# Two issuing queues for the loads, and a new order of words, in a fused RWKV-6 and gated state-space kernel

## Chip, cores, metric

The kernel runs on one core of one Trainium2 chip. The metric is the device time of one execution in microseconds (us). Below, PE is TensorE, PEld its weight loads, DVE VectorE, ACT ScalarE, POOL GpSimd and SP SyncE. The granted clock is the share of TensorE's full clock that the chip let it have. An engine "stands" when it is idle because its next instruction may not start yet.

## The reference

For 4 batches of 768 steps and 8 heads of 48 values, the first half is a recurrence with a decay per step (RWKV-6); its output x, 384 wide, goes through a projection, a linear scan, a gate and a second projection.

```python
for t in range(S):                                     # r, k, v, w: [4, 8, 768, 48]
    cur = np.einsum('bhd,bhe->bhde', u[None] * kt, vt)
    y[:, :, t] = np.einsum('bhd,bhde->bhe', rt, state + cur)
    state = wt[:, :, :, None] * state + np.einsum('bhd,bhe->bhde', kt, vt)
...
proj = x @ w_in                                        # 384 -> 2 x 512
val, gate = proj[..., :D_inner], proj[..., D_inner:]
for t in range(S):
    h = a[0, 0] * h + val[:, t, :]
    ys[:, t, :] = h
silu = gate * (1.0 / (1.0 + np.exp(-gate)))
return silu * ys @ w_out
```

## The kernel before

The sequence is cut into 12 segments of 256 steps (two chunks of 128). Everything the kernel does is a word of one long list; the words run through a small interpreter, and each engine executes its own words strictly in list order. `ld.4.w` loads w of segment 4, `ld.4.v.1` one half of v, `lw` a part of a weight matrix; `Q`, `K`, `ru`, `vc`, `dv` are products and casts whose letter after the colon names the engine (d, p or a); `y.6` is DVE's sum of chunk 6; `op`, `osb`, `ship` are the last product, its copy out of PSUM and its transfer to the output.

```python
ORDER = """
ld.0.w.1 ld.0.w.0 ldu ld.0.k.1 ld.0.r.1 ln.0.1 cs.0.P.1:0 ld.0.k.0 cs.0.N.1:1 ex.0.P.1 ln.0.0
ld.0.r.0 ex.0.N.1 tot.0:2 cs.0.P.0:0 ld.1.w cs.0.N.0:1 ex.0.P.0 Q.0.1:d ex.0.N.0 E.0 K.0.1:d
... (54 lines cut; 733 words in all)
"""
class InOrder:                       # each engine keeps the order of the list
    def __getattr__(self, name):
        op = getattr(self.engine, name)
        return lambda *args, **kwargs: self.tc.keep_in_program_order(op(*args, **kwargs))
...
    qp = ring("qp", NB, [C, G, H, DP], BF16)
    kp = ring("kp", NB, [C, G, H, DP], BF16)
    loaded = {x: ring(x, 6, [C, G, H, D], F32) for x in "rkvw"}
...
    def ld_(m, name, g=None):
        T[name, m] = loaded[name][m % 6]
        if g is None:                # w: a whole segment, runs of 384 bytes
            sp.dma_start(out=pairs(T[name, m]), in_=...)
            return
        sp.dma_start(out=T[name, m][:, g], in_=...)   # a half: runs of 192 bytes
...
    for word in ORDER.split():
        word, _, place = word.partition(":")
        fn, *args = word.split(".")
        ...
        work[fn](*(int(a) if a.isdigit() else a for a in args), **given)
```

Of the kernel before, what the change touches and what calls it, by code (L numbers as in the profile page):

```python
# [528 lines left out]
```

## Time and profile before

| | before |
|---|---|
| median of 3 runs | 151.3 us (150.02 to 151.83) |
| span of the profiled run, mean granted clock | 149.1 us, 0.973 |
| busy us: PE, DVE, ACT, POOL | 121.3, 123.2, 104.3, 87.7 |

### The profile page before, as it was taken

How to read it: one execution, taken by the hardware profiler on the slowest of the kernel's cores; microseconds unless marked ns; L12 is line 12 of the kernel's file. 1: busy time of each engine (PE TensorE's matmuls, PEld its weight loads, DVE VectorE, ACT ScalarE, POOL GpSimd, SP SyncE). 2: the span in 40 equal slices, each digit the busy share in tenths (PEclk: the TensorE clock that was granted, in tenths of full speed). 3: DMA queues.
4: the chain of work that ended last, by engine and by line, in shares of the span. 5: the costliest groups of instructions: out<-in, count | busy, mean ns of one | idle time of the engine just before them, and what ended most of it. 6: DMA issues, size and time to landing. Idle time of an engine off the chain costs nothing.

```text
span 149.1 us, 3917 instructions
## 1 busy us (share of the span) xinstructions
PE 121.3 (81%) x1560; PEld 83.8 (56%) x1560; DVE 123.2 (83%) x171; ACT 104.3 (70%) x186; POOL 87.7 (59%) x82
## 2 busy tenths in 40 slices
PE   0436985759996779998879799999697999999990
PEld 0124643435574546786547578777444677777760
DVE  3049649998559999899999999999869999989930
ACT  3725566845858898799968899889544785655471
POOL 7801627059629939687139699629699429194100
PEclk9999999999999999999999999999857999999998
DMA  4999999999799999899898998999991211301235
GB/s 93 193 228 202 202 159 257 228 205 255 135 206 206 167 234 254 174 209 313 164 208 185 210 199 180 276 203 197 241 254 38 98 67 52 110 0 57 106 135 181
DMA packets 94690, 26.40 MB, mean 177 GB/s; under 512 B 89424, under 2 KB 94672, under 8 KB 94672
## 3 DMA queue, kind: packets, MB, share of 16 engines
q1 hardware_dynamic: 94672, 26.16, 85.1%
q8 instruction: 12, 0.20, 0.7%
q14 instruction: 6, 0.05, 0.1%
HBM read 21.43 MB, written 4.72 MB: 175 GB/s over the span
## 4 chain that ended last, share of the span: by engine, by line
PE 31%; SPq 26%; DVE 20%; DMA 9%; issue 6%; ACT 3%; POOL 3%; DVEq 0%; ACTq 0%; POOLq 0%
SPq L100 26%; PE mm L100 20%; PE yk L100 6%; DVE rk L100 6%; DVE hT L100 5%; DVE At L100 4%; DMA r<-in_r_dram 4%; DMA v<-in_v_dram 3%; PE trp L100 3%; DMA k<-in_k_dram 3%; DVE y L100 2%; PE att L100 2%; DVE kp L100 1%; POOL kp L100 1%; ACT z L100 1%
## 5 line engine op out<-in xcount | busy, mean ns | idle before, releaser
L100 PE MATMUL mm<-xT,w_in_sb 128*128 128x256 bf16 x288 | 38.1, 277 | 1.5 <-DVE hT L100 0.7
L100 PEld LDWEIGHTS <-w_in_sb 128*128 128x128 bf16 x288 | 26.9, 99 | 7.1 <-issue 3.3
L100 DVE TENSOR_TENSOR At<-att,mask 128x1024 bf16<-128x1024 f32 x24 | 29.1, 1212 | 0.6 <-PE att L100 0.6
L100 ACT COPY QK<-trp 128x1024 bf16<-128x1024 bf16 x24 | 24.3, 1012 | 7.2 <-PE trp L100 6.9
L100 POOL TENSOR_TENSOR qp<-r,P 128x768 bf16<-128x768 f32 x10 | 19.4, 1940 | 15.9 <-DMA r<-in_r_dram 11.0
L100 POOL TENSOR_TENSOR dv<-v,dvec 128x768 f32<-128x768 f32 x12 | 18.3, 1526 | 9.4 <-DMA v<-in_v_dram 3.5
L100 DVE TENSOR_TENSOR_SCAN hT<-a_f,hT,mm 128x256 bf16<-128x256 f32 x32 | 22.5, 732 | 0.4 <-issue 0.2
L100 PE MATMUL mm<-w_out_sb,z 128*128 128x384 bf16 x96 | 20.0, 342 | 2.1 <-DVE z L100 1.0
L100 ACT COPY osb<-mm 128x384 f32<-128x384 f32 x24 | 11.3, 478 | 11.6 <-PE mm L100 11.5
L100 DVE TENSOR_TENSOR y<-yk,dv 128x384 bf16<-128x384 f32 x24 | 13.1, 545 | 5.9 <-PE yk L100 5.8
L100 PEld LDWEIGHTS <-QK 48*128 48x128 bf16 x352 | 11.5, 101 | 11.2 <-issue 8.2
L100 POOL TENSOR_TENSOR rk<-r,u_b 128x768 f32<-128x768 f32 x8 | 15.2, 1901 | 3.8 <-DMA r<-in_r_dram 3.8
L100 POOL TENSOR_TENSOR kp<-k,N 128x768 bf16<-128x768 f32 x8 | 15.6, 1954 | 2.5 <-DMA k<-in_k_dram 2.5
L100 DVE TENSOR_TENSOR rk<-rk,k 128x768 f32<-128x768 f32 x12 | 17.0, 1417 | 0.1
L100 ACT ACTIVATE z<-mm 128x512 bf16<-128x512 f32 x24 | 14.1, 601 | 3.4 <-PE mm L100 3.1
L100 ACT COPY xT<-trp 128x384 bf16<-128x384 bf16 x24 | 11.5, 479 | 6.8 <-PE trp L100 6.7
L100 PEld LDWEIGHTS <-kp 128*48 128x48 bf16 (+1 forms) x256 | 11.5, 109 | 8.0 <-issue 5.1
L100 PE MATMUL att<-QK 48*128 48x128 bf16 x192 | 11.0, 243 | 4.3 <-DVE At L100 3.2
L100 PE MATMUL mm<-lwp,triP 64*128 64x384 bf16 (+1 forms) x46 | 8.1, 412 | 7.3 <-ACT lwp L100 6.8
L100 ACT ACTIVATE lwp<-w 128x768 bf16<-128x768 f32 (+1 forms) x13 | 10.3, 795 | 4.8 <-DMA w<-in_w_dram 4.7
L100 PEld LDWEIGHTS <-z 128*128 128x128 bf16 x96 | 9.0, 100 | 7.9 <-issue 2.5
L100 ACT ACTIVATE P<-mm 128x384 f32<-128x384 f32 x24 | 10.9, 492 | 3.3 <-PE mm L100 3.2
(54 smaller groups left out, 201.4 us busy)
## 6 DMA issues: line engine op xcount, KB each, us to landing
k<-in_k_dram SPq DMA_DIRECT2D x24, 192.0 KB, 4.8
r<-in_r_dram SPq DMA_DIRECT2D x24, 192.0 KB, 5.0
v<-in_v_dram SPq DMA_DIRECT2D x24, 192.0 KB, 4.6
out_dram<-osb SPq DMA_DIRECT2D x24, 192.0 KB, 2.5
w<-in_w_dram SPq DMA_DIRECT2D x11, 384.0 KB, 5.0
stage<-in_moe_w_in_dram SPq DMA_DIRECT2D x4, 384.0 KB, 5.9
stage<-in_moe_w_out_dram SPq DMA_DIRECT2D x2, 384.0 KB, 5.5
w<-in_w_dram SPq DMA_DIRECT2D x2, 192.0 KB, 3.0
```

The source lines that it names most:

```text
L100: return lambda *args, **kwargs: self.tc.keep_in_program_order(op(*args, **kwargs))
```

## The change

Its intent: SP's queue holds every transfer and runs back to back (gaps of 0.04 us) to about 112 us; if ACT issues the loads of w, two queues feed the DMA. The list was worked out anew for this, with load times measured on the chip.

```diff
 ORDER = """
-ld.0.w.1 ld.0.w.0 ldu ld.0.k.1 ld.0.r.1 ln.0.1 cs.0.P.1:0 ld.0.k.0 cs.0.N.1:1 ex.0.P.1 ln.0.0
-ld.0.r.0 ex.0.N.1 tot.0:2 cs.0.P.0:0 ld.1.w cs.0.N.0:1 ex.0.P.0 Q.0.1:d ex.0.N.0 E.0 K.0.1:d
+ld.4.w lda ld.2.w ld.0.w.0 ld.0.w.1 ldu ld.0.r.1 ld.0.r.0 ln.0.0 ld.0.k.0 ln.0.1 cs.0.P.1:0
+ld.6.w ld.1.w cs.0.N.0:1 ld.0.v.0 ex.0.P.1 cs.0.N.1:2 ld.3.w cs.0.P.0:0 ex.0.N.1 Q.0.1:d
 ... (the whole list is new: the same 733 words in another order, 19 of K, Q, ru, dv, vc, z, cw on another engine)
-    qp = ring("qp", NB, [C, G, H, DP], BF16)
-    kp = ring("kp", NB, [C, G, H, DP], BF16)
+    qk = ring("qk", NB, [C, G, 2, H, DP], BF16)
+    qp, kp = [[t[:, :, i] for t in qk] for i in range(2)]
+    W_ON_ACT = (1, 2, 3, 4, 5, 6, 7, 8, 9, 10, 11)
 ...
-            sp.dma_start(
+            (act if m in W_ON_ACT else sp).dma_start(
                 out=pairs(T[name, m]),
```

(A word for a transposing DMA was added too; the list does not use it.)

More of the change, by code (lines that the diff above doesn't have):

```diff
@@ L23 @@
 ORDER = """
-ld.0.w.1 ld.0.w.0 ldu ld.0.k.1 ld.0.r.1 ln.0.1 cs.0.P.1:0 ld.0.k.0 cs.0.N.1:1 ex.0.P.1 ln.0.0
-ld.0.r.0 ex.0.N.1 tot.0:2 cs.0.P.0:0 ld.1.w cs.0.N.0:1 ex.0.P.0 Q.0.1:d ex.0.N.0 E.0 K.0.1:d
-ld.0.v.0 tr.1 ld.0.v.1 ru.0:d QK.1 ld.1.r.1 Q.0.0:d sc.1 rk.0 ln.1 ld.2.w K.0.0:d cs.1.P:01
-red.0 tr.0 ld.1.r.0 ex.1.P.0 vc.0:p At.1 ex.1.P.1 ld.1.k.0 dv.0:p QK.0 adv.0 cs.1.N:20 ld.1.k.1
-S.1 out.1 ln.2 ld.2.r.1 sc.0 y.1 tot.1:1 ex.1.N.0 Q.1:p At.0 ld.2.r.0 adv.1 E.1 yT.1 ld.2.k.1
-xT.1 S.2 out.0 ex.1.N.1 tot.2:1 ld.3.w cs.2.N:02 K.1:d ex.2.N.0 y.0 tr.2 ex.2.N.1 ld.4.w
@@ L30 @@
-cs.2.P:02 ru.2:d QK.2 ru.1:d ld.2.k.0 ex.2.P.0 tr.3 ex.2.P.1 sc.2 rk.1 ld.1.v.1 E.2 ln.3 Q.2:p
-ld.1.v.0 red.1 QK.3 cs.3.P:02 At.2 lw.0 ex.3.P.0 yT.0 tot.3:1 ex.3.P.1 rk.2 ld.3.r.1 E.3
-cs.3.N:02 xT.0 sc.3 ln.4 K.2:d ld.3.r.0 ex.3.N.0 tot.4:1 dv.1:p red.2 ld.2.v.0 tr.4 vc.1:a At.3
-ld.6.w E.4 out.2 ex.3.N.1 QK.4 cs.4.P:10 cw.0:d adv.2 ld.2.v.1 ex.4.P.0 tr.5 y.2 Q.3:p sc.4
-ex.4.P.1 S.3 lw.1 At.4 QK.5 adv.3 cs.4.N:20 ld.3.k.0 out.3 ru.3:p ex.4.N.0 sc.5 ex.4.N.1 y.3
-yT.2 ld.3.k.1 ln.6 At.5 lda vc.2:p xT.2 cs.6.P:10 S.4 pv.0.0:2 ex.6.P.0 dv.2:p ld.5.w yT.3
@@ L36 @@
-cw.1:a out.4 adv.4 ex.6.P.1 ld.4.r.0 y.4 pv.0.1:0 af K.3:p xT.3 scn.0.0 ld.4.r.1 yT.4 pv.1.1:1
-scn.0.2 xT.4 S.5 ld.4.k.1 scn.0.1 tr.6 scn.0.3 ln.5 ld.3.v.0 rk.3 QK.6 cs.5.N:20 ld.4.k.0 out.5
-scn.1.2 ex.5.N.0 tr.7 Q.4:p ld.3.v.1 sc.6 scn.1.3 ex.5.N.1 QK.7 cs.6.N:02 ld.7.w y.5 pv.1.0:1
-red.3 ru.4:p ex.6.N.0 yT.5 ld.4.v.0 At.6 ex.6.N.1 xT.5 cs.5.P:02 ld.4.v.1 scn.1.0 ex.5.P.0 sc.7
-K.4:p ex.5.P.1 ld.5.r.0 scn.1.1 vc.3:a tot.6:0 tot.5:2 ld.5.r.1 E.6 rk.4 ln.7 tr.8 ld.8.w dv.3:p
-QK.8 red.4 cs.7.N:10 adv.6 out.6 ex.7.N.0 S.7 tr.9 At.7 lw.3 dv.4:p ex.7.N.1 adv.7 E.5 cs.7.P:01
@@ L42 @@
-QK.9 ld.5.k.0 y.6 sc.8 tot.7:2 S.8 vc.4:p out.7 ex.7.P.0 At.8 ld.5.k.1 yT.6 E.7 ex.7.P.1 Q.5:p
-pv.2.1:2 ln.8 lw.2 y.7 scn.2.2 xT.6 cs.8.N:01 ld.6.r.0 cw.3:a yT.7 scn.2.3 out.8 ru.5:p sc.9
-ex.8.N.0 y.8 ld.6.r.1 adv.8 xT.7 pg.2.1:2 S.9 ex.8.N.1 At.9 ld.5.v.0 adv.9 K.5:p sl.2.1 pv.3.0:0
-ld.5.v.1 S.10 out.9 scn.3.0 yT.8 pv.2.0:1 ld.6.k.1 rk.5 xT.8 pg.0.1:2 cw.2:a scn.3.1 ld.6.k.0
-Q.6:p tr.10 sl.0.1 scn.2.0 pg.1.0:0 lw.5 QK.10 y.9 pg.2.0:2 red.5 vc.5:p lw.4 sl.1.0 yT.9 sc.10
-scn.2.1 xT.9 pg.0.0:0 ru.6:p sl.2.0 ld.9.w At.10 pg.1.1:1 sl.0.0 cs.8.P:20 sl.1.1 z.2:d ld.7.r.1
@@ L48 @@
-out.10 ex.8.P.0 rk.6 tot.8:1 adv.10 ld.7.r.0 tr.11 z.0:d ld.6.v.0 z.1:d E.8 ex.8.P.1 pv.3.1:1
-K.6:d cw.5:a ld.7.k.1 pv.4.1:0 cw.4:a scn.3.2 dv.5:p ld.7.k.0 S.11 QK.11 op.5:2 scn.4.2 ld.6.v.1
-ru.7:p scn.3.3 osb.5 tr.12 ln.9 ld.7.v.0 op.3:2 y.10 scn.4.3 op.1:1 QK.12 ld.8.r.1 Q.7:d tot.9:0
-sc.11 osb.1 yT.10 ld.10.w rk.7 osb.3 op.4:1 E.9 xT.10 cs.9.N:20 At.11 vc.6:p osb.4 tr.13
-ld.8.r.0 ex.9.N.0 pv.4.0:1 K.7:p red.6 ex.9.N.1 ld.8.k.1 adv.12 QK.13 cs.9.P:02 scn.4.0 sc.12
-ld.7.v.1 out.11 ex.9.P.0 dv.6:p S.13 tr.14 y.11 ld.8.k.0 ex.9.P.1 At.12 QK.14 op.0:0 ld.11.w
@@ L54 @@
-Q.8:p adv.13 ln.10 scn.4.1 sc.13 yT.11 out.12 S.14 osb.0 ld.9.k.0 cs.10.N:21 At.13 xT.11 op.2:0
-vc.7:p ex.10.N.0 ld.9.r.0 tr.15 y.12 osb.2 K.8:p ex.10.N.1 red.7 tot.10:0 ld.9.r.1 sc.14 E.10
-cs.10.P:12 QK.15 At.14 pv.5.1:0 ld.8.v.1 dv.7:p adv.14 ex.10.P.0 yT.12 ld.8.v.0 scn.5.2 sc.15
-ex.10.P.1 out.14 xT.12 At.15 pg.3.1:1 ru.8:p ld.9.k.1 ln.11 pv.5.0:2 y.14 sl.3.1 ship.5 tr.17
-scn.5.3 ld.11.k.1 Q.9:p out.13 scn.5.0 pg.5.1:0 ship.0 S.15 QK.17 pg.3.0:1 ship.2 scn.5.1
-ld.10.r.0 y.13 sl.5.1 pg.4.0:2 rk.8 sl.3.0 yT.13 ld.10.k.1 out.15 sl.4.0 z.3:d pg.5.0:0
@@ L60 @@
-ld.10.r.1 xT.13 ru.9:d sc.17 sl.5.0 tr.16 ship.4 op.7:1 vc.8:a At.17 K.9:p ld.10.k.0 adv.15
-QK.16 pg.4.1:2 y.15 ld.9.v.0 op.6:0 S.16 sl.4.1 rk.9 ld.10.v.0 tr.18 osb.6 sc.16 red.8 Q.10:p
-osb.7 pg.6.0:2 ld.11.k.0 QK.18 pv.6.1:0 At.16 ld.9.v.1 sl.6.0 yT.14 pg.6.1:1 dv.8:p red.9 xT.14
-ld.10.v.1 yT.15 sl.6.1 adv.16 scn.6.2 tot.11:2 ship.7 xT.15 out.16 K.10:p S.17 E.11 ship.3 sc.18
-scn.6.3 tr.19 ld.11.r.0 y.16 pv.6.0:1 At.18 QK.19 vc.9:p cs.11.P:02 ld.11.v.1 out.17 z.5:d
-ex.11.P.0 tr.20 ld.11.r.1 adv.18 scn.6.0 ru.10:p ex.11.P.1 sc.19 QK.20 ld.11.v.0 op.11:0 S.19
@@ L66 @@
-scn.6.1 adv.19 ship.6 osb.11 y.17 yT.16 cs.11.N:21 xT.16 ship.1 rk.10 out.18 op.10:0 ex.11.N.0
-ship.11 z.4:d ex.11.N.1 tr.21 osb.10 pv.7.1:1 dv.9:p At.19 QK.21 op.8:2 scn.7.2 op.9:0 z.6:p
-osb.8 y.18 vc.10:a sc.20 ship.8 yT.17 scn.7.3 pg.7.0:2 osb.9 At.20 pv.7.0:1 xT.17 ship.9 sl.7.0
-K.11:p ship.10 pg.7.1:0 S.20 scn.7.0 out.19 adv.20 red.10 yT.18 sl.7.1 op.12:2 Q.11:p scn.7.1
-xT.18 sc.21 pv.8.0:0 osb.12 y.19 vc.11:a ship.12 pv.8.1:1 S.21 scn.8.0 z.7:p yT.19 pg.8.0:2
-scn.8.2 xT.19 out.20 scn.8.1 sl.8.0 tr.22 At.21 pg.8.1:0 QK.22 dv.10:p adv.21 scn.8.3 op.13:2
@@ L72 @@
-S.22 sc.22 ru.11:p osb.13 tr.23 y.20 op.14:1 ship.13 At.22 adv.22 osb.14 out.21 rk.11 QK.23
-ship.14 pg.9.1:2 y.21 pv.9.1:1 sl.8.1 red.11 out.22 sl.9.1 sc.23 S.23 yT.20 dv.11:p pg.9.0:0
-scn.9.2 xT.20 At.23 pv.9.0:2 sl.9.0 z.8:p yT.21 op.15:0 y.22 xT.21 scn.9.3 out.23 osb.15 yT.22
-pg.10.0:1 y.23 ship.15 xT.22 scn.9.0 yT.23 pv.10.0:0 sl.10.0 scn.9.1 xT.23 op.17:1 scn.10.0
-z.9:p pv.11.0:2 osb.17 scn.10.1 op.16:1 scn.11.0 pv.10.1:0 osb.16 scn.11.1 pg.10.1:1 ship.16
-scn.10.2 ship.17 pg.11.0:2 sl.10.1 scn.10.3 pv.11.1:1 sl.11.0 z.10:d op.18:0 scn.11.2 pg.11.1:2
@@ L78 @@
-osb.18 scn.11.3 op.20:0 ship.18 sl.11.1 op.19:1 osb.20 z.11:d op.21:2 ship.20 osb.19 op.22:0
-ship.19 osb.21 op.23:1 ship.21 osb.22 ship.22 osb.23 ship.23
+ld.4.w lda ld.2.w ld.0.w.0 ld.0.w.1 ldu ld.0.r.1 ld.0.r.0 ln.0.0 ld.0.k.0 ln.0.1 cs.0.P.1:0
+ld.6.w ld.1.w cs.0.N.0:1 ld.0.v.0 ex.0.P.1 cs.0.N.1:2 ld.3.w cs.0.P.0:0 ex.0.N.1 Q.0.1:d
+ex.0.P.0 tot.0:2 ru.0:d E.0 ex.0.N.0 ld.0.k.1 K.0.0:d Q.0.0:d ld.0.v.1 tr.0 ld.1.k.0 QK.0
+ld.1.r.0 sc.0 ln.1 K.0.1:d ld.1.k.1 rk.0 af tr.1 cs.1.N:02 ld.1.r.1 red.0 vc.0:p ex.1.N.0 At.0
@@ new lines @@
+ex.1.N.1 adv.0 QK.1 cs.1.P:10 S.1 dv.0:d tot.1:2 ld.5.w out.0 E.1 ex.1.P.0 adv.1 y.0 K.1:p sc.1
+ex.1.P.1 yT.0 ld.1.v.0 At.1 ld.1.v.1 ru.1:d ln.3 Q.1:d ld.2.r.0 xT.0 cs.3.P:20 rk.1 ld.2.r.1
+tot.3:1 tr.2 ln.2 red.1 lw.0 out.1 E.3 QK.2 tot.2:1 ld.2.k.1 ex.3.P.0 tr.3 dv.1:d ex.3.P.1 sc.2
+ld.2.k.0 QK.3 y.1 vc.1:p cs.2.P:02 At.2 lw.1 ex.2.P.0 yT.1 ru.2:p ex.2.P.1 S.2 sc.3 xT.1 adv.2
+At.3 ld.9.w cs.2.N:02 cw.0:a out.2 Q.2:p ex.2.N.0 ld.3.r.1 y.2 ex.2.N.1 S.3 yT.2 E.2 adv.3
+ld.8.w ld.3.r.0 rk.2 xT.2 cs.3.N:02 out.3 K.2:d ex.3.N.0 ld.3.k.1 pv.0.0:1 cw.1:a red.2 ld.3.k.0
@@ new lines @@
+tr.4 ln.4 scn.0.0 ld.2.v.1 ex.3.N.1 y.3 QK.4 pv.0.1:0 scn.0.1 ld.2.v.0 cs.4.P:21 Q.3:p scn.0.2
+ld.10.w yT.3 sc.4 lw.3 xT.3 scn.0.3 ld.7.w ex.4.P.0 S.4 tot.4:0 At.4 tr.5 ex.4.P.1 K.3:p E.4
+cs.4.N:12 QK.5 pv.1.0:0 ld.4.r.0 ex.4.N.0 scn.1.0 tr.6 vc.2:p sc.5 ld.4.r.1 scn.1.1 QK.6 dv.2:p
+out.4 At.5 lw.2 cw.3:a sc.6 ru.3:p ex.4.N.1 y.4 tr.7 ln.5 At.6 QK.7 cs.5.P:01 ld.4.k.0 adv.4
+rk.3 pv.1.1:2 ex.5.P.0 S.5 Q.4:p yT.4 ld.4.k.1 ex.5.P.1 sc.7 xT.4 tot.5:0 At.7 out.5 ld.3.v.1
+pg.0.1:1 cw.2:a scn.1.2 ru.4:p ld.5.r.1 E.5 pg.0.0:0 ln.6 y.5 scn.1.3 yT.5 ld.3.v.0 sl.0.1 red.3
@@ new lines @@
+pg.1.1:2 ld.5.r.0 K.4:d xT.5 pg.1.0:1 ld.4.v.1 rk.4 sl.0.0 tr.8 sl.1.1 ld.4.v.0 pv.2.0:0 z.0:d
+sl.1.0 QK.8 cs.6.P:21 z.1:d scn.2.0 vc.3:p ex.6.P.0 red.4 lw.4 dv.3:p out.6 adv.6 tr.9 scn.2.1
+ld.11.w lw.5 ex.6.P.1 S.7 y.6 QK.9 adv.7 cs.5.N:01 Q.5:d ld.5.k.0 sc.8 out.7 ex.5.N.0 vc.4:p
+At.8 tot.6:2 ex.5.N.1 yT.6 ld.5.k.1 E.6 cs.6.N:01 ln.7 dv.4:p S.8 ld.6.r.0 y.7 adv.8 xT.6
+tot.7:2 S.9 ex.6.N.0 out.8 cw.4:d ld.6.r.1 sc.9 E.7 ex.6.N.1 At.9 ru.5:p cs.7.P:20 cw.5:a yT.7
+adv.9 ex.7.P.0 op.1:1 y.8 ex.7.P.1 K.5:d osb.1 ld.6.k.1 cs.7.N:02 xT.7 op.3:1 rk.5 ex.7.N.0
@@ new lines @@
+ld.6.k.0 tr.11 osb.3 S.10 ex.7.N.1 pv.3.0:1 Q.6:p red.5 ld.5.v.0 QK.11 pv.2.1:0 scn.3.0 ld.5.v.1
+tr.10 scn.2.2 ln.8 out.9 ru.6:p ld.7.r.1 scn.3.1 op.0:2 QK.10 scn.2.3 op.2:1 ld.7.r.0 osb.0 y.9
+yT.8 pg.2.0:0 osb.2 K.6:d xT.8 ld.6.v.0 pv.3.1:2 sl.2.0 rk.6 tr.12 sc.10 scn.3.2 vc.5:p pg.3.0:1
+At.10 QK.12 pg.2.1:0 dv.5:p ld.6.v.1 adv.10 sl.3.0 scn.3.3 sc.11 yT.9 ld.7.k.1 sl.2.1 pg.3.1:1
+Q.7:p At.11 xT.9 cs.8.P:20 ld.7.k.0 sl.3.1 out.10 S.11 red.6 ex.8.P.0 tr.13 ru.7:p sc.12 y.10
+tot.8:1 At.12 out.11 E.8 ld.8.r.1 QK.13 pv.4.0:1 vc.6:p y.11 ex.8.P.1 ld.8.r.0 yT.10 scn.4.0
@@ new lines @@
+dv.6:p adv.12 xT.10 out.12 S.13 cs.8.N:02 ln.9 scn.4.1 ld.8.k.0 sc.13 adv.13 K.7:p ex.8.N.0
+yT.11 y.12 tot.9:1 ld.7.v.1 xT.11 At.13 E.9 ln.10 pg.4.1:1 ld.7.v.0 z.2:d yT.12 ex.8.N.1 rk.7
+xT.12 pv.4.1:0 ld.8.k.1 sl.4.1 out.13 S.14 ru.8:p scn.4.2 ld.9.r.0 op.4:2 red.7 tr.15 ld.9.k.1
+osb.4 pv.5.0:1 Q.8:p QK.15 scn.4.3 op.5:2 ship.0 scn.5.0 vc.7:a tr.14 ld.8.v.0 y.13 pg.5.1:0
+osb.5 z.3:d ld.9.r.1 sc.15 QK.14 pg.5.0:2 scn.5.1 K.8:p At.15 sl.5.1 ld.8.v.1 yT.13 pg.4.0:1
+sl.5.0 rk.8 xT.13 cs.9.P:02 sc.14 sl.4.0 adv.14 dv.7:p At.14 ex.9.P.0 pv.6.0:1 ld.10.r.1 tr.16
@@ new lines @@
+S.15 out.14 scn.6.0 ru.9:p ship.2 adv.15 ex.9.P.1 scn.6.1 ld.9.k.0 QK.16 cs.10.P:02 y.14
+pv.6.1:1 ld.9.v.1 z.4:d ex.10.P.0 yT.14 out.15 scn.6.2 vc.8:p ex.10.P.1 sc.16 ship.1 xT.14
+cs.9.N:02 S.16 Q.9:p scn.6.3 ld.10.k.1 tr.17 ex.9.N.0 adv.16 At.16 ln.11 op.7:1 ld.9.v.0
+ex.9.N.1 S.17 osb.7 rk.9 op.8:0 ld.10.r.0 QK.17 tot.11:2 y.15 K.9:p op.9:1 ld.11.r.0 red.8 osb.8
+yT.15 out.16 E.11 osb.9 ld.10.k.0 red.9 cs.11.N:02 xT.15 sc.17 dv.8:p tot.10:1 ex.11.N.0 At.17
+tr.18 ship.7 E.10 ex.11.N.1 pv.7.0:1 ship.4 QK.18 vc.9:p y.16 cs.10.N:02 ship.5 scn.7.0 out.17
@@ new lines @@
+ex.10.N.0 ru.10:p ld.10.v.1 yT.16 adv.18 ex.10.N.1 scn.7.1 sc.18 xT.16 cs.11.P:02 ship.9 S.19
+pv.5.1:1 At.18 ship.3 ex.11.P.0 K.10:p tr.19 ex.11.P.1 ld.11.r.1 adv.19 scn.5.2 QK.19 pg.7.1:0
+ld.11.v.1 y.17 dv.9:p pv.7.1:2 sl.7.1 scn.5.3 sc.19 ship.8 yT.17 scn.7.2 op.6:1 ld.11.k.0 Q.10:p
+At.19 out.18 osb.6 pg.7.0:0 ld.11.v.0 xT.17 pg.6.1:1 scn.7.3 sl.7.0 ld.10.v.0 z.5:d tr.21 sl.6.1
+pv.8.0:2 z.7:d QK.21 ld.11.k.1 pg.6.0:0 rk.10 tr.20 ship.6 sl.6.0 y.18 Q.11:p op.10:1 scn.8.0
+QK.20 out.19 scn.8.1 op.15:0 z.6:p sc.20 y.19 osb.15 yT.18 pv.8.1:2 At.20 osb.10 xT.18 op.14:0
@@ new lines @@
+vc.10:a S.20 op.11:1 red.10 K.11:p yT.19 sc.21 osb.11 scn.8.2 adv.20 osb.14 ship.11 out.20 At.21
+xT.19 pg.8.1:1 dv.10:p tr.22 scn.8.3 pv.9.1:0 QK.22 S.21 vc.11:p pg.8.0:2 y.20 sl.8.1 scn.9.2
+sc.22 ru.11:p adv.21 sl.8.0 tr.23 S.22 op.12:1 At.22 QK.23 op.13:2 rk.11 osb.12 out.21 osb.13
+yT.20 sc.23 z.8:p scn.9.3 ship.13 pg.9.0:1 y.21 ship.12 pv.9.0:2 sl.9.0 red.11 ship.10 pg.9.1:0
+xT.20 ship.14 scn.9.0 yT.21 dv.11:p op.16:1 sl.9.1 scn.9.1 xT.21 adv.22 At.23 out.22 z.9:p
+pg.10.1:0 y.22 pg.10.0:2 sl.10.1 S.23 yT.22 out.23 sl.10.0 pv.10.1:0 osb.16 y.23 xT.22 op.19:2
@@ L80 @@
+scn.10.2 yT.23 pv.10.0:1 osb.19 scn.10.3 xT.23 op.18:2 scn.10.0 pv.11.0:0 osb.18 scn.10.1
+op.17:2 ship.18 scn.11.0 z.10:p ship.19 pv.11.1:1 osb.17 scn.11.1 ship.15 pg.11.0:2 ship.17
+scn.11.2 pg.11.1:0 sl.11.0 ship.16 scn.11.3 op.20:2 sl.11.1 op.21:1 z.11:d osb.20 ship.20
+op.22:0 osb.21 ship.21 op.23:2 osb.22 ship.22 osb.23 ship.23
 """
@@ L223, in ld_ @@
         t = {"r": r, "k": k, "v": v, "w": w}[name]
+        b, s = divmod(m, NS)
         if g is None:
-            b, s = divmod(m, NS)
-            sp.dma_start(
+            (act if m in W_ON_ACT else sp).dma_start(
                 out=pairs(T[name, m]),
@@ L349, in dv, with trd @@
             T["d", m].unsqueeze(2).to_broadcast([C, G * H, D]))
+    def trd(n):
+        m, g = divmod(n, G)
+        T["QK", n] = t = QKs[n % 3]
+        sp.dma_start_transpose(
+            out=t.rearrange("r i p c -> r (i p) c"),
+            in_=qk[m % NB][:, g].rearrange("t i h d -> t (i h d)"))
     def tr(n):
@@ L487 @@
         ld=ld_, ldu=ldu, lda=lda, lw=lw, cw=cw, af=af, ln=ln, cs=cs, ex=ex, tot=tot, E=E, K=K, Q=Q,
-        vc=vc, rk=rk, ru=ru, red=red, dv=dv, tr=tr, QK=QK, sc=sc, At=At, adv=adv, S=S, out=out_,
+        vc=vc, rk=rk, ru=ru, red=red, dv=dv, tr=tr, trd=trd, QK=QK, sc=sc, At=At, adv=adv, S=S, out=out_,
         y=y, yT=yT, xT=xT, pv=pv, scn=scn, pg=pg, sl=sl, z=z, op=op, osb=osb, ship=ship)
```

## The prediction

The "6 loads" are ACT's table loads. Rival A lost its counterargument so: it was not shown (in the changed kernel 6 of ACT's 11 issues found none of its own loads under way). Sum: from a span of 149.1 us it comes to 148.2 and then 146.9 us, with 2.2 us more for an unprofiled run to 149.1, and 148.9 was said. Its 0.7 us is an estimate from the trace of before, where rk, z, ru and kp on DVE took 10.3 us over their undisturbed times in 29 operations, all of it in nine that ran beside an operation of POOL's. That the stop at 107 us brought the half clock, on which 3.4 of its 4.8 us rest, was assumption: the trace shows the two together (a stop of 1.39 us to 107.21, half clock from 107.0 us), not that one makes the other. The "15 to 16 ns" are the median of the 192 B packets in that trace, 15 ns (mean 18).

> **What bounds the kernel now.** I read the page first, then the busy times by stretches, then the chain of waits in order of time, and last the DMA queue and TensorE around the places that the chain named. From the page, five lines:
>
> ```profile
> PE 121.3 (81%) x1560; PEld 83.8 (56%) x1560; DVE 123.2 (83%) x171; ACT 104.3 (70%) x186; POOL 87.7 (59%) x82
> ...
> DVE  3049649998559999899999999999869999989930
> ...
> PEclk9999999999999999999999999999857999999998
> DMA  4999999999799999899898998999991211301235
> ...
> PE 31%; SPq 26%; DVE 20%; DMA 9%; issue 6%; ACT 3%; POOL 3%; DVEq 0%; ACTq 0%; POOLq 0%
> ```
>
> No engine is over 83%, but the digits show who is full when: the DMA from slice 1 to slice 29 (a slice is 3.73 us, so to about 112 us), DVE from slice 9 to slice 29, and at the end DMA is nearly idle and DVE has 6 to 9 tenths. The busy times by stretches (length; then PE, PEld, DVE, ACT, POOL; clock, DMA share, GB/s) make this exact:
>
> ```profile
> 8.00:20.00 12.00, 8.21 (x105) 5.32 (x105) 8.28 (x13) 5.90 (x10) 4.07 (x3) 1.00 1.26 208
> 20.00:34.00 14.00, 9.62 (x94) 5.21 (x92) 12.70 (x12) 9.20 (x18) 5.45 (x3) 1.00 1.15 216
> 34.00:60.00 26.00, 22.32 (x333) 15.04 (x333) 21.70 (x32) 20.72 (x41) 19.36 (x13) 1.00 1.11 208
> 60.00:90.00 30.00, 27.14 (x394) 20.29 (x395) 29.08 (x40) 26.38 (x45) 20.73 (x15) 1.00 1.01 204
> 90.00:107.00 17.00, 15.07 (x228) 11.80 (x226) 16.97 (x22) 14.70 (x24) 10.84 (x7) 1.00 1.01 224
> 107.00:119.00 12.00, 10.60 (x93) 6.34 (x93) 9.96 (x10) 5.92 (x11) 10.14 (x6) 0.72 0.56 134
> 119.00:146.00 27.00, 26.55 (x318) 19.30 (x315) 23.11 (x36) 17.27 (x32) 11.01 (x6) 1.00 0.24 84
> ```
>
> So there are three stages: loads and their latency to about 34 us; DVE from 34 to 107 us (67.75 busy of 73); PE from 107 to 146 us. The hinge is at 107 us. In the chain of waits and then in PE's timeline (start, length, engine, operation) it reads:
>
> ```profile
> 101.50 4.68 DMA v<-in_v_dram
> 106.26 0.08 issue
> 106.34 0.83 POOL vb L100
> ```
>
> ```profile
> 105.58 0.25 PE L100 MATMUL yk<-s_zero,ident 128*128 128x192 bf16 x1
> 107.21 0.36 PE L100 MATMUL yk<-vb,kp 128*48 128x48 bf16 x8 [1.39 <-POOL vb L100]
> 107.50 0.61 PE L100 MATMUL att<-QK 48*128 48x128 bf16 x8
> 108.04 1.46 PE L100 MATMUL mm<-w_out_sb,z 128*128 128x384 bf16 x4
> ```
>
> A v half for segment 9 lands late, PE stands for 1.39 us, and the clock records put a granted clock of 0.5 from 107.0 to 113.8 us: the four matmuls of one output tile take 1.46 us there and 0.82 later. From 107 us on, PE hardly stops again.
>
> [...] successive r, k and v halves (192 KB) land about 1.0 us apart, a whole w (384 KB, half as many packets a byte) about 1.5 us, and where a 16 KB instruction fetch from another queue falls (19.3, 34.6, 58.6 us) landings slip by about 1 us. [...] the product rk on DVE takes 0.95 us alone and 2.78 us at 110.5 us, when a POOL product runs until 112.4. [...] the trace's 6 loads took 7.7 us, 1283 ns each.
>
> **The change part by part.**
> *Issue.* Eleven w loads leave SP's queue for ACT's. SP issues of a load take 0.43 to 0.57 us while the queue is empty (the first four) and about 1.0 us on average when it is full, which is back-pressure, since landings are 1.0 us apart as well. SP has gaps of 0.04 us only and 4 to 5 loads under way, so nothing is gained from a faster issuer. ACT pays 11 x about 0.55 = 6 us (an estimate from those first issues). The sequence of exponentials and silu switches set 8 times instead of 6: 2 x 1.28 = 2.6 us. Three casts of v leave ACT for POOL: 3 x 0.83 = 2.5 us less. ACT goes from 104 to about 110 us: still not the bound.
> *Load stream.* Same bytes[...]: it should still end at 110 to 113 us. What changes is the order. Nine shipments instead of six stand before the last load (+3 x 0.5 us), but the late segments' v come in better: the second v half of segment 9 has about ten loads behind it, not five.
> *Start.* ACT issues w of segments 4 and 2 at once, and 6, 1 and 3 as soon as segment 0's logarithms have gone through: 7.5 us of transfers beside SP's. Adding up 1.0 and 1.5 us per load, I put the first r half at about 10.5 us (8.2 now) and the second k half of segment 0 at 18 to 19 us (7.3 now). DVE is then some 5 us behind at 19 us. But it idles now between 20 and 34 us as well, and in the new list has products (ru, Q, dv of segments 0 and 1) to fill the same stretch. Tracing both lists by hand to 34 us, DVE has done 19.0 us of instructions now and about 18.2 after: +0.8 us.
> *DVE.* Counts: ru 4 to 2, Q and K one more each, dv 0 to 2: two more operations of 0.94 us, +1.9 us. [...] rk, z, ru and kp on DVE cost about 10 us over their undisturbed times in some 30 operations, so two more cost about 0.7 us.
> *Tail.* From the first matmul that needs v of segment 9, PE's instructions in list order add up to 33.6 us at full clock; it took 107.2 to 145.6 = 38.4 us. Half clock for 6.8 us is 3.4 us of that, and the stop before it 1.4 us: 4.8 us to be had if this v is early. In the new list the last loads have only 21.3 us (the first user of segment 10's v) and 19.7 us of PE work (the first transposes of k of segment 11) behind them: landing at 112 us, they end PE at about 134 us at the earliest and so bound nothing.
> *Sum.* Span 149.1 + 0.8 + 1.9 + 0.7 - 4.8 x about 0.9 = 148.2; and half of the 2.7 us that DVE idles between 40 and 50 us, mostly for a matmul result, goes with better placed loads: **146.9 us**. The unprofiled median is 2.2 us above the profiled span, which gives 149.1; I say **148.9 us**.
>
> **Rivals.**
> *A: ACT becomes a bound.* If an issue on ACT has to queue behind SP's blocked one, it costs 1 us or more, not 0.55: 11 us or more in an engine that is at 26.4 of 30 us between 60 and 90 us and stands before every decay and every copy out of PSUM. For: SP's issues stretch to 2.7 us. [...] It would make 152 to 154 us.
> *B: the early w crowd out r and k.* Then DVE never makes good its 5 us, because it has only 10 us of idle time from 20 us to its end at 143.8. For: DVE is 93% busy from 34 to 107 us. It would make 151 to 153 us.
> *C: the two queues do raise throughput*, the list fits the measured times, and the loads end some us sooner, at 105 to 108 us. Against: packets of 192 B take 15 to 16 ns an engine, back to back. It would make 144 to 147 us.
> *D: nothing moves*: another late load stops PE elsewhere and brings the half clock again. It would make 150 to 152 us.
>
> **Range and chances.** The clock episode is worth 3% in one piece, and whether one occurs is near a coin toss leaning to no. With it gone and DVE's additions absorbed, 146 to 149; with it, or under A or B, 151 to 154; C gives the low end. The 8 in 10 range is 145 to 153. Faster by over 2% means under 148.3, just below my value: 0.42. Within 2%: 0.45. Slower: 0.13, as A and B would have to come together.
>
> **What would show it.** Right: last r, k or v landing at 110 to 113 us; the k half for segment 0 near 18 us; ACT issues of about 0.55 us; 8 table loads; DVE 124 to 126 us busy; no half clock after 60 us and no PE wait over 1 us for a v there. Wrong: ACT issues over 1 us (A), DVE under 85% between 20 and 50 us (B), last landing before 108 us (C), a new half clock in the tail (D).

## More of the kernel before

The views that bound this kernel stand in the prediction. Here are only the three rows that the result will be held against: busy times by stretches of 20 us. The columns are the stretch and its length, then the busy us (and instructions) of PE, PEld, DVE, ACT and POOL, the granted clock, the DMA share and GB/s.

```profile
0.00:20.00 20.00, 10.05 (x117) 5.87 (x117) 9.71 (x23) 9.93 (x18) 10.14 (x36) 1.00 1.05 184
20.00:40.00 20.00, 15.50 (x163) 8.80 (x162) 17.41 (x18) 13.13 (x25) 10.03 (x6) 1.00 1.08 203
40.00:60.00 20.00, 16.44 (x262) 11.45 (x263) 16.99 (x26) 16.79 (x34) 14.78 (x9) 1.00 1.16 218
```

The third figure is the one to keep: DVE has done 9.71 + 17.41 + 16.99 = 44.1 us of work by 60 us. From there to the end it is busy 79.1 of 89.1 us, 89%.

## The result, and the profile after

The changed kernel took **166.72 us** (median, 165.35 to 167.76) against 150.72 us for the kernel before on the same chip. Executions over 1.5% slower than the fastest of the same kernel are left out of the means. The ratio is 1.105, 95% interval 1.093 to 1.116. (Ratios here are the mean time of one kernel's runs over that of the other's in the same rounds, so not quite the ratio of the medians quoted beside them.) The result is correct, and the profiled run, of 164.7 us span, is fast. It is slower by 10%, where 145 to 153 us had been predicted.

From the page of the changed kernel, in the order of the lines shown of before:

```profile
PE 122.1 (74%) x1560; PEld 85.4 (52%) x1560; DVE 127.3 (77%) x173; ACT 103.6 (63%) x185; POOL 87.7 (53%) x83
...
DVE  3032779887407899789699999999988999898960
...
PEclk9999999999956999555899999999969999999999
DMA  4999999999999999999989994000299210131065
...
PE 34%; DVE 28%; SPq 22%; issue 5%; DMA 5%; ACT 3%; ACTq 0%; DVEq 0%
```

Each slice is 4.12 us here. Busy times have barely changed: DVE is busy 4.1 us more, ACT 0.7 us less. So most of the 15.6 us is waiting. DVE's row shows where: a hole in slices 10 and 11, counted from 0 (41 to 49 us); after slice 1, before had none so deep. Busy by stretches:

```profile
0.00:20.00 20.00, 5.46 (x41) 2.94 (x41) 6.56 (x18) 6.21 (x12) 6.06 (x33) 1.00 1.14 197
20.00:40.00 20.00, 16.53 (x206) 10.74 (x206) 16.80 (x22) 13.86 (x27) 9.11 (x6) 1.00 1.25 215
40.00:60.00 20.00, 12.16 (x163) 8.72 (x162) 11.93 (x17) 11.38 (x21) 10.20 (x7) 0.83 1.22 220
```

DVE has 35.3 us done by 60 us, 8.8 us less than before. After that it is busy 92.0 of 104.7 us, 88%, as densely as before. So the account is short: 8.8 us behind at 60 us and 4.1 us more to do in all, 12.9 us of work, which at 88% is 14.7 of the 15.6 us. (This is an estimate from those rows. Busy time is a rough measure of work: DVE's product rk alone took from 0.94 to 2.56 us in the changed kernel.) **Most of the loss is made in the first 60 us**, 5.1 of the 8.8 us between 40 and 60 us.

What made the hole is in ACT's timeline (start, length, engine, operation; in brackets the idle time before and what ended it; ACTq is a DMA issue on ACT's sequencer):

```profile
41.35 0.48 ACT L100 COPY xT<-trp 128x384 bf16<-128x384 bf16 x1 [1.17 <-PE trp L100]
46.91 0.37 ACTq L100 DMA_DIRECT2D w<-in_w_dram  x1
47.33 0.87 ACT L100 ACTIVATE P<-mm 128x384 f32<-128x384 f32 x2 [5.50 <-DMA v<-in_v_dram]
```

ACT ended a copy at 41.83 us and then did nothing for 5.5 us. Its next word in the list is a load of w (segment 7), issued at 46.91; the exponential P behind it needs neither this w nor any v. Yet the profile names a v load as what released it, and the chain that ended last says the same (start, length, what):

```profile
38.36 8.53 DMA v<-in_v_dram
46.89 0.02 issue
46.91 0.37 ACTq L100
```

The release is a DMA of **another queue and another tensor**, and the issue follows its landing by 0.02 us. In the built program the reason can be read: the builder gives the 117 DMAs of SP and ACT together eight completion counters (the semaphores DMAHW0 to DMAHW7), in turn, in program order, and from the ninth DMA on it writes before each a wait until the previous user of its counter has landed. So this wait stands in the program itself. For the loads on ACT with a stand, program and trace give:

```
load on ACT      issued   counter's previous user   landed   ACT stood before the issue
w of segment 3   12.26    k half of segment 0       12.24    1.64 us
w of segment 5   23.16    k half of segment 1       23.14    1.50 us
w of segment 9   33.93    k half of segment 2       33.85    1.51 us
w of segment 7   46.91    v half of segment 2       46.89    5.08 us
```

ACT stands 9.7 us in all, and being in order it stands with all its exponentials and copies behind it. (The expectations below say 10.2 us: they seem to count 0.45 us in which ACT was only issuing the load before.) On SP the same wait costs next to nothing: at most 5 of its loads are under way when it issues the next, fewer than the 8 counters, and in the changed kernel a single issue of SP's follows such a landing (43.41 after 43.39 us).

SP's timeline shows one more oddity:

```profile
97.41 0.72 SPq L100 DMA_DIRECT2D k<-in_k_dram  x1
117.35 1.32 SPq L100 DMA_DIRECT2D out_dram<-osb  x3
```

SP stands 19.2 us at a shipment whose product is not ready, with the last seven loads behind it; they land at 121.8 to 129.9 us, and the DMA row shows the gap in slices 24 to 28. This looked like a second culprit.

### The profile page after: what moved, and what is told of

It is laid out like the page before. It is cut to its first block, busy times and chain, and to the rows that moved or that the text cites. A ratio compares the mean times of both kernels' runs of the same rounds, so it can differ in the third digit from the quotient of the medians.

```text
span 164.7 us, 3900 instructions
## 1 busy us (share of the span) xinstructions
PE 122.1 (74%) x1560; PEld 85.4 (52%) x1560; DVE 127.3 (77%) x173; ACT 103.6 (63%) x185; POOL 87.7 (53%) x83
## 4 chain that ended last, share of the span: by engine, by line
PE 34%; DVE 28%; SPq 22%; issue 5%; DMA 5%; ACT 3%; ACTq 0%; DVEq 0%
SPq L100 22%; PE mm L100 22%; DVE hT L100 7%; PE yk L100 6%; DVE At L100 5%; DMA v<-in_v_dram 5%; DVE rk L100 5%; PE trp L100 4%; DVE y L100 3%; DVE z L100 3%; PE att L100 2%; DVE dvec L100 2%; DVE S L100 1%; DVE qk L100 1%; ACT QK L100 1%
## 5 line engine op out<-in xcount | busy, mean ns | idle before, releaser
L100 PE MATMUL mm<-xT,w_in_sb 128*128 128x256 bf16 x288 | 38.7, 280 | 4.5 <-DVE hT L100 4.0
L100 POOL TENSOR_TENSOR dv<-v,dvec 128x768 f32<-128x768 f32 x10 | 15.4, 1538 | 23.4 <-DVE dvec L100 20.0
L100 PEld LDWEIGHTS <-qk 128*128 128x128 bf16 (+1 forms) x352 | 18.4, 110 | 13.4 <-issue 8.8
L100 POOL TENSOR_TENSOR rk<-r,u_b 128x768 f32<-128x768 f32 x10 | 18.8, 1880 | 3.9 <-DMA r<-in_r_dram 3.9
L100 POOL CAST vb<-v 128x768 bf16<-128x768 f32 x10 | 10.7, 1072 | 18.6 <-DMA v<-in_v_dram 18.6
L100 POOL TENSOR_TENSOR qk<-r,P 128x768 bf16<-128x768 f32 x9 | 16.3, 1814 | 6.2 <-ACT P L100 3.7
L100 PE MATMUL trp<-ident,qk 128*128 128x128 bf16 x192 | 17.8, 244 | 2.4 <-DVE qk L100 2.1
L100 POOL TENSOR_TENSOR qk<-k,N 128x768 bf16<-128x768 f32 x7 | 13.1, 1877 | 10.4 <-DMA k<-in_k_dram 6.6
L100 DVE TENSOR_TENSOR rk<-rk,k 128x768 f32<-128x768 f32 x12 | 17.6, 1464 | 0.0
L100 ACT ACTIVATE N<-mm 128x384 f32<-128x384 f32 x24 | 11.3, 489 | 9.8 <-PE mm L100 7.6
L100 PEld LDWEIGHTS <-QK 48*128 48x128 bf16 x352 | 11.9, 104 | 10.3 <-issue 6.3
```

## The experiments

The first four runs set the two halves of the change apart: list and queue. All are built from the changed kernel with only the list or `W_ON_ACT` edited.

### The list of before, all on SP

```diff
-ORDER = """ (new list)      -W_ON_ACT = (1, 2, ..., 11)
+ORDER = """ (list of before) +W_ON_ACT = ()
```

> Control: the changed kernel's code with the joint q and k tile, but the list of before and every load on SP. All theories: 150 to 152 us, as before, with the 11 w loads landing at the same places. If it is over 153, the layout of the joint tile costs something by itself.

Measured: 152.54 us against 153.3 us, ratio 1.000 (0.991 to 1.010). The joint tile for q and k costs nothing measurable. In the profiled run the clock was half from 19.9 to 43.8 us, and at 151.40 us it was still the shortest of the four; two runs with mean clocks of 0.966 and 0.977 took 152.33 and 153.09 us. Half clock this early was hidden.

### The list of before, w on ACT

```diff
+ORDER = """ (list of before)    # W_ON_ACT stays (1, ..., 11)
```

> The list of before, w on ACT. Theory 1 (ACT, in order, stands at the issue of a w load until an older load, which used the same one of 8 completion counters, has landed): the counters as built put the w of segment 8 behind the second half of the output weights stage 2, which landed at 62.0 us in the run of before, while ACT reaches that issue at 52.8; segment 6 waits some 2 us and segment 4 about 1 us: ACT stands about 8 to 12 us, time 156 to 163 us. Theory 2 (the new list alone is bad, the queue is harmless): 150 to 152 us.

Measured: 158.60 us, ratio 1.036 (1.024 to 1.048). So the queue alone costs about 4%. The time fell where theory 1 put it, but not for its reason: ACT stands at its counters for only 3.1 us here (1.08 and 2.05 us), not 8 to 12. Besides, each w but the first is issued 0.5 to 7.9 us later than with the same list on SP, because ACT reaches the word later than SP did, and ACT then waits 9.1 us for w instead of 4.9. How the 4% is shared between stands and lateness is not shown.

### The new list, all on SP

```diff
-W_ON_ACT = (1, 2, 3, 4, 5, 6, 7, 8, 9, 10, 11)
+W_ON_ACT = ()
```

> The new list, every load on SP. Theory 1: the four stands of ACT (1.6, 1.5, 1.5 and 5.1 us in the changed kernel's trace, 9.7 us) and the half clock after them go: 152 to 157 us. Theory 2 (the early w in the new list crowd out r and k, and the list is bad whatever the queue): 162 to 168 us. Theory 3 (shipments that stand in SP's queue ahead of the last seven loads): its part, some 3 to 6 us, stays in either case, with an idle DMA of over 10 us near 100 us.

Measured: 162.68 us, ratio 1.065 (1.057 to 1.073). The list alone costs about 6.5%, and 1.065 x 1.036 = 1.103 is nearly the whole 1.105: the two parts add up. (That may be partly chance: the queue costs about the same with both lists, though ACT stands 3.1 us with one and 9.7 us with the other.) Its busy times by stretches:

```profile
0.00:20.00 20.00, 4.07 (x32) 2.26 (x32) 4.51 (x16) 6.14 (x11) 6.10 (x33) 1.00 1.06 195
20.00:40.00 20.00, 17.20 (x206) 10.81 (x207) 17.26 (x22) 13.14 (x26) 7.64 (x5) 1.00 1.22 217
40.00:60.00 20.00, 16.57 (x198) 11.40 (x196) 15.58 (x22) 15.04 (x26) 12.42 (x8) 0.83 1.02 205
```

DVE has 37.4 us by 60 us: the deep hole is gone with ACT's stands, but the start is 5.2 us behind before.

### The new list, only the w loads on ACT that need not stand

```diff
-W_ON_ACT = (1, 2, 3, 4, 5, 6, 7, 8, 9, 10, 11)
+W_ON_ACT = (4, 2, 6, 1, 11)
```

> The new list, only the w of segments 4, 2, 6, 1 and 11 on ACT, whose counters had been released long before ACT came to them; those of 3, 5, 9, 8, 10 and 7 on SP at the same places of the list. Theory 1: like the new list with all on SP, 152 to 157 us. If the queue as such cost something, it would lie between that and 166.7. Theory 2: 162 to 168 us.

Measured: 163.43 us, ratio 1.069 (1.058 to 1.081), as on SP alone within the noise; none of ACT's issues waits for a counter. So five loads on ACT's queue cost nothing measurable. This fits the counters, but it also takes six loads away, so it is not yet a proof.

### The new list on SP, the early w loads put back

```diff
-ld.4.w lda ld.2.w ld.0.w.0 ...  ld.6.w ld.1.w ... ld.3.w ... ld.0.k.1
+lda ld.0.w.0 ... ld.0.k.1 ... (w of segments 4, 2, 6, 3, 5 moved 14 to 85 words back, the loads behind them forward)
```

> New list, all loads on SP, with only the early w put back: w of 4, 2, 6 and 3 leave their places ahead of segment 0 and 1's r, k and v. Theory B (early w crowd out r and k, and DVE never makes it good): DVE's busy time in the first 20 us rises from 4.5 to 8 us or more, and the time falls from 162.7 to 156 to 159. If the start is made good later anyway: 161 to 164.

Measured: 164.0 us against 151.91 us, ratio 1.089 (1.081 to 1.098): no gain, although the start was repaired. DVE has 10.8 us done at 20 us (4.5 in the list as it was), but 37.2 us at 60 us (37.4): in the middle other loads come late (POOL stands 9.5 us for one half of r, until 41.2 us), and the lead is lost again.

### The new list on SP, six shipments moved behind the last loads

```diff
-... ship.7 ... ship.4 ... ship.5 ... ship.9 ... ship.3 ... ship.8 ... ld.11.k.1
+... ld.11.k.1 ship.7 ship.4 ship.5 ship.9 ship.3 ship.8
```

> New list, all loads on SP, with six shipments (7, 4, 5, 9, 3, 8) moved behind the last seven loads. Theory 3 (loads held behind a shipment that waits for its data): the 13 us of idle DMA from 103 to 116 us go, the last load lands near 112 instead of 129 us, the half clock at 103 us goes, and the time falls to 157 to 160. If the loads held were not needed earlier, since DVE and PE are full there: 161 to 164.

Measured: 162.65 us, ratio 1.081 (1.070 to 1.092), again no gain. The edit did what it should; the DMA rows of the list as it was and of this run (slices of 4.03 us):

```profile
DMA  4999999999899899989989999200099700140165
```

```profile
DMA  5999999999999899989999999990080100040165
```

The loads no longer stop in slice 25 to resume in slice 29: they run on and end near 109 us instead of 129 us, and the time is the same. SP's stand of 19 us is a striking sign and not a cause: the time does not hang on when those loads land.

### The new list on SP, loads in the order of their first use

Only SP's words move: each load to its rank by the first word that uses it, shipments from the fourth on behind the loads.

```diff
-... ld.9.w ... ld.8.w ld.3.r.0 ... ld.2.v.1 ... ld.2.v.0 ... ld.10.w ... lw.3 ... ld.7.w ...
+... (v of segment 2 first; w of 9, 8, 10, 7, 11 and the second weights where they are used)
```

> New list, all loads on SP in the order of their first use in the list, shipments behind the last load except 0, 1 and 2; the streams of ACT, DVE, PE and POOL unchanged. If SP's order is the whole loss of the list (theories B and 3): 150 to 155 us. If the new order and split of the work on the engines is at fault: 158 us or more.

Measured: 157.07 us, ratio 1.040 (1.027 to 1.053), 5.6 us less than the run before it on the same chip. Busy times:

```profile
0.00:20.00 20.00, 8.77 (x89) 4.93 (x90) 11.30 (x24) 9.06 (x18) 9.32 (x35) 1.00 1.10 185
20.00:40.00 20.00, 17.13 (x213) 11.41 (x213) 15.37 (x22) 14.29 (x28) 8.92 (x6) 1.00 1.05 202
40.00:60.00 20.00, 14.84 (x192) 10.72 (x185) 16.99 (x22) 15.21 (x24) 14.85 (x10) 0.77 1.15 237
```

DVE has 43.7 us by 60 us, almost before's 44.1. So **the order of the loads over the whole first 60 us** is about 4 points of the list's cost. (The run before it already had the shipments at the end, and they gave nothing.) Repairing only its start or only its end gave nothing.

### The list of before with w on ACT, eight w loads issued earlier

```diff
-ld.1.w to ld.8.w where SP had them
+each 7 to 35 words earlier in the list (4 to 8 of ACT's instructions)
```

> Old list, w on ACT, with eight w issues moved four to eight ACT instructions earlier. In the run with the old list on ACT the stands were 3.1 us only (1.1 and 2.1 us), and each w was issued 1 to 9 us later than SP had issued it. Theory 1b (on ACT a load cannot run ahead of the stream; it is issued when ACT gets there, too close to its use): 151 to 154 us, ratio 0.99 to 1.015. If the cost is that of issuing on ACT or of the shared counters: 157 to 160 as before.

Measured: 156.99 us (154.01 to 158.09), against 151.91 us; only one of the four runs counts as fast, the one of 154.01 us, so there is no ratio. Its trace is worth something still: earlier words did not give earlier loads. ACT's stands rose from 3.1 to 9.9 us, and the issues came 0.02 us after their counters' earlier users had landed (38.58 after 38.56, 55.57 after 55.55, 29.77 after 29.75 us). The lateness of w was traded for stands; the run neither confirms nor excludes a share for lateness in the old list.

### Fewer DMAs, so that the counters reach further back: on SP

To make the counters' wait vanish without taking a needed wait away, r, k and v of segments 1 to 11 are loaded by one DMA each. That works only in w's arrangement of rows, so both of these runs give a wrong result, with the same engine instructions and bytes.

```diff
+        if m and name != "w":
+            if (name, m) in both:
+                return                  # the second half's word does nothing
+            both.add((name, m))
+            g = None                    # one DMA for the whole segment
         if g is None:
```

> The new list with all loads on SyncE, and r, k and v of segments 1 to 11 loaded by one DMA each in place of two (in w's arrangement of rows, so the result is wrong on purpose; 33 DMAs fewer, the same engine work and bytes). It is the yardstick of the next run. The eight completion counters now reach back over about twice as much work. Expected 1.03 to 1.07 of before (the new list on SyncE with the halves apart measured 1.065), somewhat less if the longer descriptors move faster.

Measured: 162.25 us against 151.69 us, ratio 1.073 (1.066 to 1.079). This is the yardstick. (For the "longer descriptors": in the trace of before a w, 384 KB in runs of 384 bytes, lands about 1.5 us after the load ahead of it, and two halves, 192 KB each in runs of 192 bytes, take about 2.0 us.)

### Fewer DMAs, w on ACT

```diff
-W_ON_ACT = ()
+W_ON_ACT = (1, 2, 3, 4, 5, 6, 7, 8, 9, 10, 11)    # on top of the run before
```

> The same with the w loads on ScalarE. Counters theory: the 3.5% to 4% of the queue change is ScalarE standing until the earlier user of a shared completion counter has landed; with half as many DMAs that user is long done, ScalarE's stands add up to under 3 us (10.2 us in the changed kernel) and the time is within 1% of the merged kernel on SyncE. Rival (w loads on a second queue harm by themselves, through contention, early transfers or issue cost on ScalarE): 3% to 4% above the merged kernel on SyncE all the same.

Measured: 163.64 us, ratio 1.077 (1.070 to 1.083). The step from SP to ACT, 3.7% with the halves apart, is 0.4% here, within the noise. ACT's timeline where the deep hole was:

```profile
43.91 0.48 ACT L100 COPY xT<-trp 128x384 bf16<-128x384 bf16 x1 [1.30 <-PE trp L100]
43.92 0.43 ACTq L100 DMA_DIRECT2D w<-in_w_dram  x1
44.39 0.87 ACT L100 ACTIVATE P<-mm 128x384 f32<-128x384 f32 x2
```

The same copy, the same w of segment 7, the same exponential, and no stand: the load is issued 0.01 us after the copy begins. The counter's previous user is now a load of k for segment 3, landed at 35.6 us. One issue still stands, for 0.6 us, instead of 9.7 us in all. All eleven w loads are on ACT, as in the changed kernel, so the queue as such and the issue time cost nothing measurable. The counters' wait is shown with one reserve: with fewer, longer DMAs the queues are less busy too (DMA share 0.99 from 40 to 60 us, 1.22 in the changed kernel), so contention of the two queues is also weaker here. It looks small: with the halves apart, v of segment 2 lands at 44.4 and 46.9 us with w on ACT and at 44.0 and 45.3 us without.

### The list of before on SP, v of segment 9 earlier

```diff
-... ship.5 ... ld.11.k.1 ... ship.0 ... ld.9.v.0 ... ld.11.k.0 ... ld.9.v.1
+... ld.9.v.0 ... ld.9.v.1 ... ld.11.k.1 ... ship.0 ...
```

> The list of before on SyncE with one change: the two v loads of segment 9 are issued seven and five DMAs earlier, so they land near 97 us and not 106.2. The prediction's tail claim: PE's stop of 1.39 us and the half clock at 107.0 to 113.8 us go, worth 0.99 to 0.97 of before (up to 4.8 us off). Rival: the stop or the half clock turns up elsewhere, or VectorE is as late anyway, 0.995 to 1.01 of before.

Measured: 153.29 us, ratio 1.009 (1.003 to 1.015): no gain, a small loss if anything. The two halves land at 96.7 and 98.8 us (102.8 and 106.2 before), and the half clock at 107 us is gone, as the clock row shows:

```profile
PEclk9999999999999999999999999999999599999999
```

But in PE's timeline other stops have taken the old one's place:

```profile
107.41 0.28 PE L98 MATMUL yk<-S,QK 48*128 48x48 bf16 x8 [1.50 <-DVE y L98]
...
116.37 1.52 PE L98 MATMUL mm<-w_out_sb,z 128*128 128x384 bf16 x8 [2.12 <-DVE z L98]
```

PE waits 1.50 us and 2.12 us for DVE, and a short half clock (117.7 to 121.1 us) follows the second. The first of these stops was made by the edit itself. Two loads went forward in a full queue, so ten other DMAs went back, among them the last half of r for segment 10, which landed at 103.36 us instead of 99.67. POOL's product with this r stands ahead of a dv that DVE's y needs. POOL in the kernel before, then POOL and DVE in this run:

```profile
99.83 1.82 POOL L100 TENSOR_TENSOR qp<-r,P 128x768 bf16<-128x768 f32 x1 [3.47 <-DMA r<-in_r_dram]
```

```profile
103.52 1.81 POOL L98 TENSOR_TENSOR qk<-r,P 128x768 bf16<-128x768 f32 x1 [6.00 <-ACT xT L98]
...
106.80 0.56 DVE L98 TENSOR_TENSOR y<-yk,dv 128x384 bf16<-128x384 f32 x1 [1.44 <-POOL dv L98]
```

In both runs the product starts 0.16 us after that r has landed (the name xT in brackets is the profile's guess at the releaser). So one late load was traded for another, as rival D said. The run does not show what the tail is worth when every load is in time.

### The new list on SP by first use, with before's split of work

```diff
-dv.0:d K.1:p Q.1:d dv.1:d vc.1:p ru.2:p cw.0:a K.4:d ...
+dv.0:p K.1:d Q.1:p dv.1:p vc.1:a ru.2:d cw.0:d K.4:p ...   (19 words)
```

> The new list with SyncE's loads in order of first use (measured 1.040 of before) and the 19 words of K, Q, ru, dv, vc, z and cw that the new list gave to another engine given back to the engine of the list of before. If the split of work is the rest of the list's cost: VectorE's busy time falls from 126.2 to 123 or 124 us, and the time to 1.00 to 1.02 of before. If it is the new order of the engines' work itself: 1.03 to 1.05.

Measured: 155.37 us, ratio 1.027 (1.022 to 1.032). DVE is busy 125.5 us (126.2). The ratio is lower than the 1.040 of the run by first use, but on another chip, and the intervals overlap; the split is worth about a point by the means and 0 to 3 by the intervals. In its trace stood one conspicuous stop of PE:

```profile
59.67 0.32 PE L98 MATMUL yk<-S,ident 128*128 128x192 bf16 x1 [4.28 <-DVE y L98]
```

DVE had two z products (4.2 us) and some smaller work ahead of the sum y of chunk 6, whose inputs were ready near 54.5 us.

### As before it, with the y of chunk 6 ahead

```diff
-... z.1:d scn.2.0 ... red.4 ... scn.2.1 ... S.7 y.6 QK.9 adv.7
+... S.7 y.6 scn.2.0 z.1:d red.4 scn.2.1 QK.9 adv.7
```

> The new list with loads by need and the old split (measured 1.027 of before), with one more edit: on VectorE the y of chunk 6 goes ahead of one z product, one reduction and two scans that stood before it. If the 4.28 us stop of TensorE and the half clock behind it are the rest of the list's cost: the stop is under 1 us and the time 0.99 to 1.01 of before. If it is hidden or only moves: 1.02 to 1.03, with another stop of several us within the next 20 us.

Measured: 154.26 us against 150.97 us, ratio 1.027 (1.020 to 1.034): nothing gained. That stop shrank, and another took its place:

```profile
55.27 0.24 PE L98 MATMUL yk<-S,ident 128*128 128x192 bf16 x1 [0.36 <-DVE y L98]
58.03 0.82 PE L98 MATMUL mm<-lwp,triN 64*128 64x384 bf16 x4 [2.30 <-DVE hT L98]
```

So the stop of 4.28 us was not itself the loss. The rest of the list's cost, 2.7%, stays open. DVE is busy 1.9 us longer (125.1 against 123.2 us), but that is no proof: DVE's busy time for the very same words of the list of before was 119.2 us in one run (w on ACT) and 123.3 us in another (v of segment 9 earlier).

### The list of before on SP, loads in order of first use

```diff
-... ldu ld.0.k.1 ld.0.r.1 ... ld.4.w ld.2.k.0 ... ship.5 ld.11.k.1 ship.0 ship.2 ...
+... ld.0.r.1 ld.0.k.1 ldu ... ld.2.k.0 ld.4.w ... (six shipments behind the last load)
```

> The list of before on SyncE, its 100-odd DMAs alone put in the order in which the list first uses what they load, six results sent later. If the order of loads still costs something in before, VectorE's sum at 40 us rises above 27.1 us and the time is 0.97 to 0.99 of before; if before's order is as good, 0.99 to 1.01.

Measured: ratio 1.008 (0.998 to 1.018) from two runs; the other four slow, one of them, the profiled one, at 206.64 us with PE busy for 184 us. No gain can be read from it. No version that was run beats the kernel before.

## Why the prediction was wrong, and where it was right

**Start, and with it the load stream: the first failed step.** The prediction followed both lists by hand to 34 us, got 19.0 us of DVE work against 18.2, and charged 0.8 us. In the traces DVE has 22.4 us done at 34 us before and 18.7 after: 3.7 us. At 20 us DVE was 3.2 us behind, less than the 5 us said; what failed is the catching up, since from 20 to 34 us it did 12.2 us of work against 12.7 before. The hand count for the kernel before already missed its own trace by 3.4 us, which could have been seen beforehand. And it stopped at 34 us, though the new list went on pulling w of segments 8, 9, 10, 7 and the later weights ahead of v of segments 2 and 3. From 34 to 60 us DVE lost a further 5.1 us (21.7 to 16.6; part of it is ACT's stand). New order by first use, with nothing else touched, gives back 5.6 us. "Half of the 2.7 us goes with better placed loads" had the wrong sign.

**Issue: the second failed step, an unpriced wait.** The price of an issue was right: 0.37 to 0.65 us were measured for 0.55, and rival A's long issues did not come: ACT's issue at 46.91 us took 0.37 us inside one of SP's of 2.08 us (from 45.63). What was left out is that the wait for a shared completion counter moves with the issue. It was in the sum nowhere. With the new list it makes 9.7 us of stands; moving w to ACT costs 3.7% with them and 0.4% nearly without. With the old list the same move costs 3.6% with 3.1 us of stands, and there w also came late, which the sum left out too. Rival A had the right engine and the wrong mechanism: ACT was not the bound by work (103.6 us busy, not 110), it was held.

**Tail: the third failed step.** The sum took 4.8 us as to be had with v of segment 9 early, as if nothing else became late by it. In the one run that tried, r of segment 10 landed 3.7 us later, POOL stood 6.0 us for it, PE stopped again, and the time was 1.009. In the changed kernel this v landed at 98.5 us, and a half clock came in the tail all the same (120.5 to 123.9 us). Rival D said just this. Whether the 4.8 us can be had with all loads in time stays open; DVE, busy 14.80 of 15 us from 115 to 130 us in the kernel before, leaves little room for it.

**Rival B** was close in its mechanism: DVE never made good what it lost early, for want of idle time after 60 us (88% to 89% busy in both kernels), and its sign came: from 20 to 50 us DVE was busy 19.8 of 30 us, 66% (though the 85% that was named could not tell, since the kernel before had 24.8 us there, 83%). It was sized from the start alone, at 151 to 153 us, and the loads of the middle were not counted; repairing the start alone indeed gained nothing.

**DVE's own work** was roughly right: +2.6 us predicted; +3.0 us in the new list on SP and +4.1 us in the changed kernel. **The sum** ends with 149.1 us worked out and 148.9 us said, without a reason given; nothing hangs on it.

**Signs.** The k half of segment 0 landed at 17.4 us (18 to 19 said), the first r half at 10.2 us (10.5): the transfers' arithmetic held. The two queues raised no throughput worth the name (197, 215 and 220 GB/s in the first three stretches of 20 us; 195, 217 and 205 with the same list on SP alone): rival C is out. The 8 table loads came, 1.28 us each. The last loads landed at 129.9 us and not 110 to 113, through SP's stand at a shipment, a sign that went wrong at no cost. No half clock after 60 us was wrong, too: 65.9 to 79.5 and 120.5 to 123.9 us. The joint tile cost nothing, as assumed.

In all: 3 to 4 points of the 10.5 are the counters, about 4 the order of the loads, and about 3 the rest of the new order and split, which is not explained. (These come from different chips, so each is good to about a point.)

## What to carry to other kernels

Before moving a DMA to a compute engine, ask not what its issue costs but what it must wait for before it may be issued, completion counters included (here 0.37 to 0.65 us an issue, and 9.7 us of stands); on an in-order engine everything behind stands with it. A new order of loads is judged by following the full engine's sum of finished work against the old one through the whole stretch until nothing idles any more, not to the end of the start-up, and a hand count is first checked against the trace that exists. The longest stop in a trace may be one that nobody was waiting for: SP's 19 us was taken away and the time stayed. PE's stops of 1.4 and 4.3 us were taken away too, and each time another came in their place: in a full queue a load put forward puts others back (two v halves forward, r of segment 10 back by 3.7 us), so ask of every repair what it makes late.
